# A linear-attention and gated-MLP block: the first two denominators on a bank pair of the queries, two gated rows in buffers of their own, one partial-product buffer for the late input pairs, and a new order table

## The chip, the cores and the metric

The kernel runs on one core of a Trainium2 chip. The engines named below are TensorE (PE, its weight loads PEld), VectorE (DVE), ScalarE (ACT), GpSimd (POOL) and SyncE (SP), which here issues nearly all transfers. The metric is the time of one execution in device microseconds; the lower, the better.

## The reference

The input x has 2048 rows of 512. Two residual blocks follow one another, the first a linear attention with 32 heads of 16, the second an MLP whose gate mixes the rows.

```python
phi = lambda t: where(t > 0, t + 1, exp(t)) + 1e-06
q, k, v = heads(layernorm(x) @ wqkv)
kv  = einsum('bhsd,bhse->bhde', phi(k), v);  z = einsum('bhsd->bhd', phi(k))
num = einsum('bhqd,bhde->bhqe', phi(q), kv); den = einsum('bhqd,bhd->bhq', phi(q), z)
h   = x + (num / den) @ wo
z   = gelu(layernorm(h) @ w_in);  z1 = z[..., :896];  z2 = layernorm(z[..., 896:])
g   = einsum('ts,bsf->btf', w_sp, z2) + b_sp
out = h + (z1 * g) @ w_out
```

The gelu is the tanh form; all inputs are bf16.

## The kernel before, in words

Rows come in 16 tiles of 128, or in 4 groups of 512 (GW). Everything between the loads and the last stores stays on the chip. The stages, with the times of the profile:

- 0 to 42: k units (two tiles each: norm, transposes, the product with wqkv, phi, then the outer product of pk and xn, L692) with the query units of the first two row groups between them. A query unit q_unit(tg, c) makes half of the queries of a row group, 2 × 128 columns, on two PSUM banks that next_pair() hands out by turns. It is named q12 and so on by tg and c. Its phi is an exponential on ACT (e), a clamp of e (L614) and a combination (L619) on DVE.
- 42 to 72: z_unit (L714) sums pk, DVE turns this into zc (zred, zT, zc, L718 to L721). The denominators: for each row group tg a product of zc and pqT (L824) on bank 6, its reciprocal on ACT by a logarithm (r) and an exponential (rcp), four SP transfers that spread rcp over the partitions (spread, L815), and two DVE multiplications of pqT (L840). Beside that: the four outer products are copied to ct by ACT, multiplied with the value columns of wqkv (L790), masked (kvm, L794) and multiplied with wo; the four results are copied to m by ACT and DVE (L801). Then, tile by tile, o_n: pqT times m, plus x by DVE (h, L852), row statistics by ACT (sh) and POOL, the norm by DVE (hn), and an SP transpose hnT.
- 72 to 140: the MLP's input products. Both w_in halves are multiplied by a scheme of two-by-two sums: hn_sums and w_sums build sums (hs, ws) on DVE; cell3 and cell2 run the products over a bank and its neighbour, ACT copies partial products into buffers p5z, and add_on (L882) adds them. cell2 makes z1 for two tiles at a time by z1_half: an ACT copy with gelu into z1t. The pairs of tiles 6, 7 and of 14, 15 (cell2_3 and cell2_7, the list ZLATE) come late, in the middle of the first mix block. Until then they alternated between p5z0 and p5z1.
- 105 to 212: the 2048 × 2048 mix in blocks mix(ia, ib, nest, early), the first of them early. The same two-by-two scheme is applied, partly twice (nested, with quarter sums nu of the weights, nv of z2 and adds at L1051). u_sums and comb (L755) build the weight sums in DVE, over the 16 transposed weight tiles wt. gate (L1019) and gate_p (L1030, L1031) add bias and the other partial result and multiply z1t in place; then an SP transpose makes zgT.
- 176 to 222: the output product with w_out, again by sums (us of zgT, vs of w_out by wout_sums), plus h, and stores.

The order of all operations on all engines is one table of numbers, ORDER, which schedule() decodes; waits follow from the data's hazards. So an engine runs its list in turn, and whatever waits holds up what is behind it. Many buffers share space: vs0 and vs1 lie where the upper parts of wt0 and wt1 were, and the nu buffers lie over wo and the space behind it.

Of the kernel before, what the change touches and what calls it, by code (L numbers as in the profile page):

```python
# [11 lines left out]
P = 128  # L12
GRAN = 16
EARLY = 0
SEM_NS = 45.0
# [1236 lines left out]
```

## Time and profile before

| | us |
|---|---|
| median of 3 runs (lowest, highest) | 224.12 (224.12, 224.31) |
| the profiled execution's own time | 224.06 |
| its span | 222.2 |
| busy PE, DVE, ACT, POOL | 215.1, 203.1, 142.7, 50.5 |
| granted TensorE clock | 1.00 |

The span runs from the first to the last instruction; the profiled run's own time has 1.9 us more around it. TensorE has 1334 matmul records of 1346, so a gap of about 0.2 us in a run of matmuls can be a record that is missing. In the rows of the timeline an engine's successive instructions overlap: of a DVE row of 0.62 us some 0.54 us pass until the next can start, of a TensorE group of 0.55 us some 0.39. In the chain of waits PE has 83% of the span, DVE 7%, ACT 3% and DMA 3%, of which 5.56 us are the first load of x.

### The profile page before, as it was taken

The numbers are of one execution on the slowest core, as the hardware profiler recorded it, in microseconds if no ns is written. First come the engines' busy times: TensorE is split into PE (matmuls) and PEld (weight loads), VectorE is DVE, ScalarE is ACT, GpSimd is POOL, SyncE is SP. The second block draws the span as 40 slices with busy tenths as digits, with TensorE's granted clock in tenths as the row PEclk, the third lists the DMA queues.
The fourth block names the chain that finished last, engine by engine and source line by source line (L and its number), as shares of the span: only waits on it lengthen the run. The fifth ranks groups of instructions, "written<-read, shape, count | busy, mean of one in ns | idle before, by whom it ended". The sixth has DMA issues, their size and how long they took to land.

```text
span 222.2 us, 3846 instructions
## 1 busy us (share of the span) xinstructions
PE 215.1 (97%) x1334; PEld 123.3 (56%) x1346; DVE 203.1 (91%) x472; ACT 142.7 (64%) x283; POOL 50.5 (23%) x133
## 2 busy tenths in 40 slices
PE   7999999999999999999999999999999999999995
PEld 6444444453334444444545555756766778767764
DVE  3899858969999999999999999997999998999895
ACT  5887654299789999999764646716385265533330
POOL 3444400000665655868700000000000000000000
PEclk9999999999999999999999999999999999999999
DMA  5758877928866553205994434986247024037274
GB/s 180 248 109 242 164 158 169 238 64 193 182 144 126 108 120 81 42 0 94 168 169 156 96 74 104 177 165 126 49 81 138 1 41 86 1 72 110 61 201 142
DMA packets 75026, 27.12 MB, mean 122 GB/s; under 512 B 64768, under 2 KB 75008, under 8 KB 75008
## 3 DMA queue, kind: packets, MB, share of 16 engines
q1 hardware_dynamic: 74304, 26.30, 55.7%
q10 hardware_dynamic: 704, 0.59, 0.8%
q8 instruction: 10, 0.16, 0.3%
q14 instruction: 8, 0.07, 0.1%
HBM read 6.95 MB, written 2.10 MB: 41 GB/s over the span
## 4 chain that ended last, share of the span: by engine, by line
PE 83%; DVE 7%; ACT 3%; DMA 3%; POOL 1%; issue 1%; SPq 1%
PE psum L434 77%; PE psum L692 5%; DMA x<-in_A_x_dram 3%; DVE st L543 2%; ACT e L453 1%; DVE h L852 1%; DVE h L1188 1%; DVE psum L882 1%; DVE pqT L619 1%; SPq L464 1%; DVE pqT L840 1%; DVE pk L619 1%; ACT z1t L453 0%; POOL st L569 0%; DVE e L614 0%
## 5 line engine op out<-in xcount | busy, mean ns | idle before, releaser
L453 ACT ACTIVATE psum<-psum 128x448 f32<-128x448 f32 (+2 forms) x76 | 31.1, 426 | 32.8 <-PE psum L434 21.8
L434 PE MATMUL psum<-z,wt 128*128 128x448 bf16 (+1 forms) x216 | 41.7, 335 | 0.1
L434 PEld LDWEIGHTS psum<-z,wt 128*128 128x128 bf16 x216 | 20.9, 98 | 15.4 <-DVE z L588 0.3
L434 PE MATMUL psum<-win,hnT 128*128 128x448 bf16 x112 | 26.4, 353 | 0.0
L453 ACT ACTIVATE z1t<-psum 128x448 bf16<-128x448 f32 (+1 forms) x24 | 16.4, 684 | 9.8 <-PE psum L434 7.6
L453 ACT ACTIVATE e<-psum 128x1024 bf16<-128x1024 f32 (+1 forms) x18 | 16.7, 929 | 9.2 <-PE psum L434 8.7
L434 PE MATMUL psum<-ws,hs 128*128 128x448 bf16 x72 | 18.9, 353 | 0.0
L434 PEld LDWEIGHTS psum<-win,hnT 128*128 128x128 bf16 x112 | 10.4, 98 | 11.0 <-ACT z L453 0.9
L434 PE MATMUL psum<-zt,sa 128*128 128x448 bf16 (+1 forms) x92 | 16.5, 316 | 0.0
L434 PE MATMUL psum<-m,pqT 128*128 128x512 bf16 x63 | 15.0, 380 | 1.0 <-DVE pqT L840 0.9
L882 DVE TENSOR_TENSOR psum<-psum,p5z 128x448 f32<-128x448 f32 x24 | 15.1, 628 | 0.6 <-ACT z1t L453 0.4
L453 ACT ACTIVATE z<-psum 128x896 bf16<-128x896 f32 x16 | 15.1, 979 | 0.7 <-PE psum L434 0.7
L692 PE MATMUL psum<-pk,xn 128*128 128x512 bf16 x63 | 15.2, 379 | 0.2 <-DVE pk L617 0.2
L434 PE MATMUL psum<-wqkv,xnT 128*128 128x512 bf16 x62 | 14.9, 379 | 0.4 <-DVE pqT L619 0.3
L434 PE MATMUL psum<-xnT,wqkv 128*128 128x512 bf16 x62 | 15.0, 379 | 0.2 <-issue 0.2
L453 ACT ACTIVATE p<-psum,b 128x448 f32<-128x448 f32 x22 | 13.2, 637 | 2.4 <-DVE u L1030 1.4
L1030 DVE TENSOR_TENSOR u<-psum,p 128x448 bf16<-128x448 f32 x22 | 13.6, 620 | 1.0 <-PE psum L434 0.6
L434 PE MATMUL psum<-nv,nu 128*128 128x224 bf16 x108 | 14.4, 259 | 0.1
L567 POOL TENSOR_SCALAR st<-st 128x1 f32<-128x1 f32 x10 | 4.8, 484 | 37.0 <-ACT sh L453 31.5
L543 DVE BATCH_NORM_STATS2 st<-x 128x6 f32<-128x512 bf16 x15 | 9.8, 678 | 3.7 <-DMA x<-in_A_x_dram 3.7
L434 PE MATMUL psum<-wout,zgT 128*128 128x256 bf16 (+1 forms) x71 | 12.8, 295 | 0.2
L614 DVE TENSOR_SCALAR e<-e 128x1024 bf16<-128x1024 bf16 (+1 forms) x18 | 6.9, 388 | 5.8 <-ACT e L453 5.8
(155 smaller groups left out, 459.7 us busy)
## 6 DMA issues: line engine op xcount, KB each, us to landing
r<-rcp SPq DMA_DIRECT2D x16, 128.0 KB, 2.8
out_dram<-h SPq DMA_DIRECT2D x15, 128.0 KB, 1.8
win<-in_B_w_in_dram SPq DMA_DIRECT2D x4, 448.0 KB, 3.8
x<-in_A_x_dram SPq DMA_DIRECT2D x6, 256.0 KB, 3.7
wqkv<-in_A_wqkv_dram SPq DMA_DIRECT2D x2, 512.0 KB, 4.9
wout<-in_B_w_out_dram SPq DMA_DIRECT2D x1, 896.0 KB, 5.0
wt<-in_B_w_sp_dram SPq DMA_TRANSPOSE x32, 4.0
wo<-in_A_wo_dram SPq DMA_DIRECT2D x1, 512.0 KB, 6.6
```

The lines of the kernel that those rows point to most:

```text
L434: inst = pe.matmul(out_ap, lhsT=a, rhs=b, start=start and i == 0, stop=stop and i == len(pairs) - 1, **kw)
L453: return g.add("ACT", lambda ac: ac.activation(out_ap, in_ap, func, **kw), [in_ap, *extra], [out_ap] + ([accum] if accum is not None else []),
L464: return g.add(eng, lambda q: q.dma_start(out_ap, in_ap), [in_ap], [out_ap], cost=issue, lat=lat, dma=name, **k)
L543: dve(lambda v: v.bn_stats(s[:, 0:6], src[:, n, :]), [src[:, n, :]], [s[:, 0:6]], D)
L567: pool(lambda p: p.tensor_scalar(s[:, 2:3], s[:, 0:1], s[:, 0:1], -1.0 / (n * n), op0=ALU.mult, op1=ALU.mult), [s[:, 0:1]], [s[:, 2:3]], 240)
L614: dve(lambda v: v.tensor_scalar(e, e, 1.0, EPS_PHI, op0=ALU.min, op1=ALU.add), [e], [e], w * GW, acc=4)
L619: dve(lambda v: v.scalar_tensor_tensor(dst, t, 1.0 + EPS_PHI, e, op0=ALU.add, op1=ALU.max), [t, e], [dst], w * GW, ps=True)
L692: inst = pe.matmul(bank(CB[c]), lhsT=xn[:, i, c * P:(c + 1) * P], rhs=pk[:, i, :], start=i == 0, stop=i == NT - 1)
L840: dve(lambda v, q=q, r=r: v.tensor_tensor(q, q, r, ALU.mult), [q, r], [q], 2 * GW, acc=2)
L852: dve(lambda v, n=n, b=b, s=s: v.scalar_tensor_tensor(h[:, n, :], bank(b), 1.0, x[:, n, :], op0=ALU.mult, op1=ALU.add, accum_out=s[:, 0:1] ...
L882: dve(lambda v: v.tensor_tensor(half(b), half(src), p, ALU.add), [half(src), p], [half(b)], HW, ps=True)
L1030: dve(lambda v: v.tensor_tensor(u, half(b), p, ALU.add), [half(b), p], [u], HW, ps=True)
```

## The change

Four edits, with no instruction more or less on any engine.

1. The denominator code becomes a function den(tg, db). Row groups 0 and 1 are now called ahead of the copies to ct, on the two banks that next_pair() gives; groups 2 and 3 follow the query units on bank 6, as before.
2. The gates of rows 8 and 9 in the early mix block write to buffers gt0 and gt1, and the transposes zgT8 and zgT9 read these. gt0 and gt1 lie where vs0 and vs1 are written later, so vs0 now follows the transpose of row 8, vs1 that of row 9. z1t8 and z1t9, whose space the copies z1t14 and z1t15 of the late pair take, are free earlier.
3. cell2_3 and cell2_7 both use p5z0; the nu1 buffers swap places by twos (k ^ 2).
4. A new ORDER table.

In the diff the code between the denominators and the query units (ct copies to m, L776 to L805) is left out where it only moves.

```diff
--- before.py
+++ after.py
@@ -13,7 +13,7 @@
 GRAN = 16
 EARLY = 0
 SEM_NS = 45.0
-ORDER = "c-jTQ0{|EY5Cp)zz5Up>8{4+i#<p#{v28WBZQHhO
+ORDER = "c-jrsg92EG76ibvyXVHXZQE&V+qP}nwr!hjY@2Ot
 
 
 class _Op:
@@ -350,6 +350,7 @@
     N4 = HT // 2 * (HW // 2) * 2
     o_up = [o_wsp + n * S * 2 + ZR for n in (0, 1, HT, HT + 1)]
     assert V3 + HF * P * 2 + ZR <= S * 2 and 2 * V3 + 8 * D + 4 * N4 + 2 * S // 2 <= NT * D * 2
+    gt = {HT + c: g.sbuf(f"gt{c}", o_up[c], [FH], BF16) for c in (0, 1)}
     vs = [g.sbuf(f"vs{k}", o_up[k], [HF, D // 2], BF16) for k in range(4)]
     us = [[g.sbuf(f"us{c}{k}", o, [HF, P], BF16) for k, o in enumerate(os)]
           for c, os in enumerate(([o + V3 for o in o_up], [o_pk + k * HF * P * 2 for k in range(4)]))]
@@ -357,7 +358,7 @@
     o_n = o_pk + 2 * V3 + 8 * D
     nv5 = [g.sbuf(f"nv5{k}", o_n + k * N4, [HT // 2, HW // 2], BF16) for k in range(4)]
     nv1 = [g.sbuf(f"nv1{k}", o_win + k * N4, [HT // 2, HW // 2], BF16) for k in range(4)]
-    nu1 = [g.sbuf(f"nu1{k}", o_wo + k * S // 2, [HT // 2, P], BF16) for k in range(4)]
+    nu1 = [g.sbuf(f"nu1{k}", o_wo + (k ^ 2) * S // 2, [HT // 2, P], BF16) for k in range(4)]
     np1 = g.sbuf("np1", o_ct + 3 * TB, [HW // 2], FP32)
     np5 = g.sbuf("np5", o_win + KD * FH * 2 + 3 * S, [HW // 2], FP32)
     assert o_ct + 3 * TB + HW * 2 <= cur[0] and 3 * S + HW * 2 <= KD * FH * 2 and S // 2 <= NT * 16 * 4
@@ -776,37 +777,7 @@
     u_sums(0, sae[:2])
     u_sums(1, sae[2:])
 
...
-    DB, MERGE, PM = 6, (), ()
+    MERGE, PM = (), ()
 
     def spread(tg, c, w):
         i = tg % 2
@@ -814,9 +785,8 @@
         src_ap = bass.AP(src.tensor, src.offset, [list(src.ap[0]), [0, 4], [1, w * GW]])
         g.add("SP", lambda q: q.dma_start(dst, src_ap), [rcp[:, i:i + w, :]], [dst], cost=700, lat=2200, dma=f"r{tg}{c // 2}")
 
-    for tg in range(NG):
+    def den(tg, db):
         tok = slice(tg * GW, (tg + 1) * GW)
-        db = DB
 
         def fn(pe, tok=tok, db=db):
             inst = None
@@ -838,6 +808,42 @@
                         pool(lambda v, q=q, r=r: v.tensor_tensor(q, q, r, ALU.mult), [q, r], [q], 1800)
                     else:
                         dve(lambda v, q=q, r=r: v.tensor_tensor(q, q, r, ALU.mult), [q, r], [q], 2 * GW, acc=2)
+
+
+    db = next_pair()
+    for tg in (0, 1):
+        den(tg, db + tg)
+
...
+    while qs:
+        q_unit(*qs.pop(0))
+    for tg in range(2, NG):
+        den(tg, 6)
 
 
     AB, HPAIR = [4, 5, 7], 2
@@ -1010,25 +1016,27 @@
     for q in ZPRE:
         cell2(q, win1, wq1[0], 6, 7, p5z[q % 2], z1_half)
 
-    def gate(n, c, b):
+    def gate(n, c, b, to=None):
         o = z1[n][:, c]
+        d = o if to is None else to[:, c]
         if GACT:
             u = u_t[cnt[0] % len(u_t)]
             cnt[0] += 1
             act(u, half(b), ACT.Identity, HW, bias=b32[:, n:n + 1], extra=[b32[:, n:n + 1]])
-            dve(lambda v: v.tensor_tensor(o, u, o, ALU.mult), [u, o], [o], HW, acc=2)
+            dve(lambda v: v.tensor_tensor(d, u, o, ALU.mult), [u, o], [d], HW, acc=2)
             return
-        dve(lambda v: v.scalar_tensor_tensor(o, half(b), b32[:, n:n + 1], o, op0=ALU.add, op1=ALU.mult),
-            [half(b), b32[:, n:n + 1], o], [o], HW, ps=True)
+        dve(lambda v: v.scalar_tensor_tensor(d, half(b), b32[:, n:n + 1], o, op0=ALU.add, op1=ALU.mult),
+            [half(b), b32[:, n:n + 1], o], [d], HW, ps=True)
 
     cnt = [0]
     GACT = True
 
-    def gate_p(n, c, b, p):
+    def gate_p(n, c, b, p, to=None):
         o, u = z1[n][:, c], u_t[cnt[0] % len(u_t)]
+        d = o if to is None else to[:, c]
         cnt[0] += 1
         dve(lambda v: v.tensor_tensor(u, half(b), p, ALU.add), [half(b), p], [u], HW, ps=True)
-        dve(lambda v: v.tensor_tensor(o, u, o, ALU.mult), [u, o], [o], HW, acc=2)
+        dve(lambda v: v.tensor_tensor(d, u, o, ALU.mult), [u, o], [d], HW, acc=2)
 
     HQ, H4 = HW // 2, HT // 2
 
@@ -1119,13 +1127,14 @@
             gate_p(tl, hi, E, pa)
             dma_t(zgT[tl], z1[tl], f"zg{tl}", issue=1300, lat=1750)
             matmuls(half(B), [(wt[th][:, s, :], z2[:, s, hi]) for s in ss], **onto)
-            gate_p(th, hi, B, pb)
+            to = gt[th] if early else None
+            gate_p(th, hi, B, pb, to)
             if nest & 16:
                 act(p2[c], half(B), ACT.Identity, HW, bias=b32[:, th:th + 1], extra=[b32[:, th:th + 1]])
                 continue
             matmuls(half(B), [(wt[th][:, HT + s, :], zt4[:, s, :]) for s in ss], **onto)
-            gate(th, lo, B)
-            dma_t(zgT[th], z1[th], f"zg{th}", issue=1300, lat=1750)
+            gate(th, lo, B, to)
+            dma_t(zgT[th], gt[th] if early else z1[th], f"zg{th}", issue=1300, lat=1750)
         if nest & 16:
             nested(SETS[0] + 2, SETS[1] + 2, wt[ia + HT][:, HT:NT, :], wt[ib + HT][:, HT:NT, :], zt4, nu2, nv4, np1)
             for i, c in sets:
@@ -1199,7 +1208,7 @@
         mix(MIX[k], MIX[k + 1], NEST[k // 2], k == 0)
         if k == 0:
             for q in ZLATE:
-                cell2(q, win1, wq1[0], 6, 7, p5z[q % 2], z1_half)
+                cell2(q, win1, wq1[0], 6, 7, p5z[0], z1_half)
             load_wout()
             for n in W4:
                 load_w(n)
```

What the new order does at three places. First ACT, from the query unit q12 on: ct are the copies of the outer products, e the exponentials of query units, r and rcp a denominator's two passes. Before:

```order
L453 ACTIVATE e_192<-psum 128x1024
L453 ACTIVATE ct<-psum 128x512 x4
L453 ACTIVATE e_192<-psum 128x1024
L453 ACTIVATE r<-psum,epst 128x512
L453 ACTIVATE rcp<-r 128x512
L453 ACTIVATE e_191<-psum 128x1024
L453 ACTIVATE r<-psum,epst 128x512
L453 ACTIVATE rcp<-r 128x512
```

Now:

```order
L454 ACTIVATE e_194<-psum 128x1024
L454 ACTIVATE r<-psum,epst 128x512
L454 ACTIVATE rcp<-r 128x512
L454 ACTIVATE r<-psum,epst 128x512
L454 ACTIVATE ct<-psum 128x512 x3
L454 ACTIVATE e_194<-psum 128x1024
L454 ACTIVATE ct<-psum 128x512
L454 ACTIVATE e_193<-psum 128x1024
L454 ACTIVATE rcp<-r 128x512
```

Both r and the first rcp moved ahead of the copies, and q22's exponential ahead of the fourth copy. On SP the spreads follow rcp. On DVE q12's phi moved ahead of zred, kvm behind q20's phi.

Second, DVE around the late pair of tiles 14 and 15; the two rows with p5z are its adds (cell2_7), gt0 the gate of row 8, nv are quarter sums. Before:

```order
L1019 TENSOR_TENSOR z1t8_69<-u0_134,z1t8_69 128x448
L755 TENSOR_TENSOR sa01_125<-sa00_124,wt2_82 128x1024
L1030 TENSOR_TENSOR u0_134<-psum,p511_131 128x448
L755 TENSOR_TENSOR nu52_172<-sa00_124,sa10_126 128x512
L755 TENSOR_TENSOR nv10_160<-z2_53 128x896
L755 TENSOR_TENSOR nv11_161<-z2_53,nv10_160 128x896
L755 TENSOR_TENSOR nv50_156<-zt0_77 128x896
L755 TENSOR_TENSOR nv51_157<-zt0_77,nv50_156 128x896
L1031 TENSOR_TENSOR z1t9_70<-u0_134,z1t9_70 128x448
L882 TENSOR_TENSOR psum<-psum,p5z1_133 128x448
L1019 TENSOR_TENSOR z1t9_70<-u1_135,z1t9_70 128x448
L755 TENSOR_TENSOR vs0_140<-wout_187 128x768
```

Now:

```order
L1026 TENSOR_TENSOR gt0_140<-u0_134,z1t8_69 128x448
L1038 TENSOR_TENSOR u0_134<-psum,p511_131 128x448
L1039 TENSOR_TENSOR gt1_141<-u0_134,z1t9_70 128x448
L756 TENSOR_TENSOR nu52_174<-sa00_124,sa10_126 128x512
L756 TENSOR_TENSOR nv10_162<-z2_53 128x896
L756 TENSOR_TENSOR nv50_158<-zt0_77 128x896
L756 TENSOR_TENSOR nv11_163<-z2_53,nv10_162 128x896
L756 TENSOR_TENSOR wt11_91<-wt3_83,wt11_91 128x1024
L756 TENSOR_TENSOR vs0_142<-wout_189 128x768
L888 TENSOR_TENSOR psum<-psum,p5z0_132 128x448
L756 TENSOR_TENSOR nv51_159<-zt0_77,nv50_158 128x896
L756 TENSOR_TENSOR nv12_164<-z2_53 128x896
```

The sum into wt11 and vs0 moved ahead of the pair's first add, nv51 and the last part of row 9's gate behind it; sa01 stands earlier, ahead of cell2_3's second add. On PE one short group of the mix (nu50) moved ahead of the group that waits for the first add, and one (nu11) ahead of the group that waits for the second. On SP the second part of wt7 now goes ahead of zgT8, and zgT9 behind four more weight loads.

Third, DVE in the second mix block (rows 7 and 4), around nu22, a quarter sum of wt7 and wt4; z1t10 is the gate of row 10. Before:

```order
L1019 TENSOR_TENSOR z1t10_71<-u2_136,z1t10_71 128x448
L755 TENSOR_TENSOR nv20_173<-z2_53 128x896
L755 TENSOR_TENSOR nu22_183<-wt7_87,wt4_84 128x512
L1030 TENSOR_TENSOR u1_135<-psum,p510_130 128x448
L755 TENSOR_TENSOR nu20_181<-wt4_84 128x512
```

Now:

```order
L1059 TENSOR_TENSOR psum<-psum,np5_171 128x224
L756 TENSOR_TENSOR sa10_126<-wt14_94 128x1024
L756 TENSOR_TENSOR nu12_168<-wt5_85,wt6_86 128x512
L756 TENSOR_TENSOR nu22_185<-wt7_87,wt4_84 128x512
L756 TENSOR_TENSOR nu52_174<-sa00_124,sa10_126 128x512
```

nu22 moved behind work of the third block (rows 5 and 6: wt5, wt6, wt14), while its product on PE moved ahead of the two long products of wt7 and wt15.

54 lines of the change are left out of this document (27 added, 27 removed).

## The prediction

> **What bounds the kernel now.** I read the totals first, then the chain of waits, then busy time by stage, then single stretches of the timeline.
>
> ```profile
> span 222.2 us, 3846 instructions
> PE 215.1 (97%) x1334; PEld 123.3 (56%) x1346; DVE 203.1 (91%) x472; ACT 142.7 (64%) x283; POOL 50.5 (23%) x133
> ```
>
> TensorE is busy in 97% of the span, VectorE in 91%. The change adds and removes no instruction on any engine, so all that it can win is time in which TensorE stands still, and all that it can lose is new standing still. Whether busy matmul time has slack of its own is read from one row:
>
> ```profile
> 132.68 1.68 PE L434 MATMUL psum<-zt,wt 128*128 128x448 bf16 x8
> 134.19 0.54 PE L434 MATMUL psum<-win,hnT 128*128 128x448 bf16 x2
> 134.94 0.55 PE L434 MATMUL psum<-zt,sa 128*128 128x224 bf16 x4
> 135.33 0.55 PE L434 MATMUL psum<-nv,nu 128*128 128x224 bf16 x4
> 136.03 0.55 PE L434 MATMUL psum<-win,hs 128*128 128x448 bf16 x2 [0.16 <-DVE psum L882]
> 137.18 0.55 PE L434 MATMUL psum<-z,wt 128*128 128x224 bf16 x4
> 137.89 0.55 PE L434 MATMUL psum<-ws,hnT 128*128 128x448 bf16 x2 [0.16 <-DVE psum L882]
> ```
>
> Eight matmuls of 448 columns take 134.19 − 132.68 = 1.51 us from start to start, 189 ns each: 2.4 columns per ns, hence no slack inside a group. A short group takes 0.39 (134.94 to 135.33). By that step the group at 136.03 could have started at 135.72 and the one at 137.89 at 137.57: two stalls of 0.32 each, both ended by the add of L882.
>
> The Trainium skill (Perfetto Trace Analysis, Identifying the Most-Contended Engine) warns that busy matmul time says little about the roofline and names the share of the weight loads instead. By that rule the 56% of PEld would leave room inside the 97%, and the sum would be free to fall by more than the stalls. The step of 189 ns speaks against it here.
>
> The chain shows where TensorE is not in front (start, us, what):
>
> ```profile
> 56.03 0.63 ACT sh L453 x2
> 57.10 1.05 POOL st L569
> 58.23 0.51 POOL st L570
> 58.82 0.59 POOL rs L583
> 59.84 1.83 DVE h L852 x6
> 62.93 71.81 PE psum L434 x372
> 134.77 0.55 ACT z1t L453
> 135.34 0.64 DVE psum L882
> ```
>
> Behind the head these are the two places: the denominators (51 to 63; the statistics of POOL, h and the scalings of L840 stand in front there) and the late input pair (134.8 to 137.9). By stage (PE, PEld, DVE, ACT, POOL busy, then clock, DMA share, GB/s):
>
> ```profile
> 41.00:63.00 22.00, 20.84 (x125) 8.46 (x126) 19.43 (x39) 17.73 (x32) 4.53 (x9) 1.00 0.73 155
> 125.00:140.00 15.00, 14.68 (x96) 8.71 (x94) 14.49 (x31) 8.58 (x19) 0.00 (x0) 1.00 0.54 107
> 140.00:160.00 20.00, 20.00 (x141) 13.33 (x139) 18.31 (x45) 8.70 (x20) 0.00 (x0) 1.00 0.68 128
> ```
>
> Here 22.00 − 20.84 = 1.16 us are lost on PE around the denominators and 0.32 in the late pair (the rows' ends are modelled, so the start-to-start sum, 0.64, is the better one). From 140 on PE loses nothing, and DVE has 1.69 us to spare.
>
> **Denominators.** Nothing new is computed; r, rcp and eight SP transfers move ahead of the ct copies.
>
> ```profile
> 17.00 1.90 PE L434 MATMUL psum<-wqkv,xnT 128*128 128x512 bf16 x7 [0.31 <-DVE pqT L619]
> 41.28 1.05 PE L714 MATMUL psum<-pk,ones 128*32 128x512 bf16 x16
> 42.53 0.68 DVE L718 TENSOR_REDUCE zred<-psum 128x128 f32<-128x512 f32 x1
> 43.59 0.29 DVE L721 TENSOR_TENSOR zc<-zT,selm 128x128 bf16<-128x128 f32 x1
> 44.20 2.07 ACT L453 ACTIVATE ct<-psum 128x512 bf16<-128x512 f32 x4 [2.65 <-PE psum L692]
> 46.12 1.05 ACT L453 ACTIVATE e<-psum 128x1024 bf16<-128x1024 f32 x1
> 47.03 0.72 ACT L453 ACTIVATE r<-psum,epst 128x512 f32<-128x512 f32 x1
> 47.78 0.63 ACT L453 ACTIVATE rcp<-r 128x512 bf16<-128x512 f32 x1
> 48.44 5.24 SPq L815 DMA_DIRECT2D r<-rcp  x8
> r<-rcp SPq DMA_DIRECT2D x16, 128.0 KB, 2.8
> 48.98 0.69 DVE L794 TENSOR_TENSOR kvm<-psum,bmask 128x512 bf16<-128x512 f32 x1
> 50.04 1.22 DVE L619 SCALAR_TENSOR_TENSOR pqT<-psum,e 128x1024 bf16<-128x1024 f32 x1
> 54.12 3.63 PE L434 MATMUL psum<-m,pqT 128*128 128x512 bf16 x16
> 58.10 1.04 PE L434 MATMUL psum<-m,pqT 128*128 128x512 bf16 x4 [0.36 <-DVE pqT L840]
> ```
>
> Before, eight issues take 5.24, so the fourth starts at 48.44 + 3 × 0.655 = 50.4 and lands some 2.8 later, at 53.2; the scaling of pqT after it lets o_0 start at 54.12. Now z_unit goes ahead of one product of k12 and starts near 40.2, with 0.2 won in the head (a product of 0.86 stands ahead of the group that waited for pqT at 17.00). DVE has q12's phi behind it by 41.7; zred to zc take 43.59 + 0.29 − 42.53 = 1.35, to 43.05; den_0 follows and r begins near 43.45, not 47.03. The transfers then land 3.6 earlier, by 49.7, and no longer bind. What binds instead: the copies start behind r, rcp and the second r, 0.72 + 0.63 + 0.72, the last of them from 44.7 on when den_1 is through, so the third ends near 46.9; q22's exponential (0.93 a step) is put ahead of the fourth, and the kv product starts near 48.4, against 48.2 for the same work before. On DVE kvm now stands behind q20's phi (1.22 and the short step on e ahead of it, 1.7 in all), and q22's phi is 0.5 late with its exponential: kvm starts near 51.1 and not at 48.98. Through wo's products and the m copies o_0 then starts near 54.55: 0.43 lost. Given back: the stall at 58.10 (DVE's scaling of the second quarter is done by then) and that before 62.93, 0.36 and 0.31 by the rows. But POOL's row statistics of o_0 begin behind an ACT pass that is now preceded by q32's second pass and q30's exponential (the 0.63 of sh ends near 57.4 and not at 56.6), and 1.05 + 0.51 + 0.59 and gaps bring the norm to 60.1, where DVE holds it ahead of o_2's h and the next scalings. So o_8 and o_9 together end near 64.6, against 64.67: −0.05, the 0.2 of the head included. Bounds: −0.55 if the norm doesn't hold DVE up, +0.4 if only o_0's lag counts. I take −0.05, since both queues are followed there row by row.
>
> The Trainium skill (PSUM — Partial Sum Buffer, PSUM bank collisions raise a hardware error) asks that two engines never meet on a bank. By that rule the borrowed query pair has a price: q22's matmuls must wait until ACT has read both denominators. By the rows r of the second ends at 45.4, as q22's second half comes up; the rule's wait is then nil, and 0.7, one r, if PE comes that much sooner.
>
> **Gate buffers, one partial buffer, nu swap.** Copies into z1t14 and z1t15 no longer wait for transposes:
>
> ```profile
> ACT z1t L453 <- DMA zgT<-z1t: 0.4, 1, 0.4
> zgT<-z1t SPq DMA_TRANSPOSE x16, 2.9
> 129.59 1.68 PE L434 MATMUL psum<-z,wt 128*128 128x448 bf16 x8
> ```
>
> That one wait of 0.4 had idle ACT time around it: 0. In exchange vs0 on DVE waits for the transpose of row 8 out of gt0, with the late pair's adds behind it. gate 8 ends near 131.0, the transfer behind one weight load on SP lands 2.9 later, near 134; vs0 comes up near 134.8: also 0, but 1.0 if the landing is as late as 135.8. The late pair's first add: from the end of wt9's product (129.59 + 1.68 = 131.3) DVE has to do four steps of 0.54 (one add, three nv), 0.32, 0.33, 0.60 (the wt11 sum) and 0.47 (vs0), 3.88 in all, to 135.2; the copy by ACT ends at 134.77 + 0.55 = 135.3, so the add still starts at 135.34. On PE one short group more stands ahead of each of the two waiting groups, 0.39 each, more than each stall of 0.32. Value: −0.64; bounds −0.64 and +0.2 (the add 0.87 later, as its place among DVE's rows alone would have it, less the 0.64).
>
> **The rest of the order.** Small swaps in 64 to 125 and 140 to 222 move producers by up to 1 us against consumers that had 0.05 to 0.5 of slack. DVE's gap below covers those after 155; for those before I put +0.1, bounds 0 and +0.6.
>
> **Sum.** The profiled run took 224.06 (span 222.2, so 1.9 around it): −0.05 − 0.64 + 0.1 = −0.59, 223.47; the median of 224.12 is 0.06 above that run, so 223.5.
>
> **Rivals.**
>
> ```profile
> 155.80 0.39 DVE L1019 TENSOR_TENSOR z1t<-u,z1t 128x448 bf16<-128x448 bf16 x1 [1.58 <-ACT u L453]
> 156.64 0.42 DVE L755 TENSOR_TENSOR nu<-wt,wt 128x512 bf16<-128x512 bf16 x1
> 170.68 0.55 PE L434 MATMUL psum<-nv,nu 128*128 128x224 bf16 x4
> ```
>
> *DVE late in the second mix block (slower).* nu22 of that block moves 10.8 us of DVE work down, its product on PE 3.0 us up. If DVE keeps its idle 1.58 at the row-10 gate, nu22 ends at 156.64 + 0.42 + 10.8 = 167.9, while PE comes for it at 167.65 less the 0.7 won: 0.9 late; the gate of row 4, moved 2.1 down and its consumer 0.4 down, then brings it to 1.5. Net +0.8: 224.9. For: DVE is 91% busy and everything there is just in time. Against: 2.9 us more of DVE work stand ahead of that gate now, which should fill the 1.58. It decides once more than 0.65 of it stays idle.
>
> *The late pair keeps its stalls (no change).* If the transpose of row 8 or the 3.88 us of DVE work run 0.3 late, PE stalls as before: −0.05 + 0.1, 224.2. For: 14.49 of 15 us busy on DVE; against: the sum above.
>
> *The norm doesn't bind (faster still).* Then −0.55 in place of −0.05: 223.0.
>
> **Chances.** Forecast 0.47, DVE late 0.30, stalls kept 0.14, norm free 0.09. About 0.2% (0.45 us) is what a measurement can tell from none, so faster begins under 223.67: 0.41 of the forecast and 0.09 make 0.50; 0.06 and 0.08 are the same; 0.30 and 0.06 slower. The range, 222.8 to 225.1, holds all but the ends of the outer cases; the forecast's own is 223.1 to 224.1.
>
> **What would show it.** Right: r ahead of ct on ACT near 43.4, o_0 near 54.5, no stall at 58.1, the two gaps at L882 gone, no idle 1.58 on DVE, PE at 20.0 of 20 after 140. Wrong: DVE waiting for zgT8 at vs0, PE waiting for nu22 near 168, or any new gap over 0.5 between 64 and 125.

## The result, and the profile after

The changed kernel took 223.26 us (223.06 to 223.64), the kernel before 224.22 beside it: ratio 0.9957, 95% interval 0.9944 to 0.9969. The forecast was 223.5. A second measurement with other runs (after_rep below) gave 223.44, ratio 0.9960, interval 0.9945 to 0.9975.

The totals of the profile after, then busy time by stage (us, then PE, PEld, DVE, ACT, POOL busy, clock, DMA share, GB/s):

```profile
span 221.6 us, 3862 instructions
PE 216.4 (98%) x1346; PEld 123.1 (56%) x1346; DVE 202.6 (91%) x472; ACT 142.6 (64%) x283; POOL 51.1 (23%) x133
```

```profile
41.00:63.00 22.00, 21.56 (x128) 8.41 (x120) 19.42 (x39) 16.84 (x29) 4.31 (x9) 1.00 0.68 147
125.00:140.00 15.00, 15.00 (x102) 9.35 (x100) 14.38 (x32) 8.46 (x19) 0.00 (x0) 1.00 0.53 99
140.00:160.00 20.00, 20.00 (x136) 13.01 (x135) 19.47 (x48) 8.90 (x20) 0.00 (x0) 1.00 0.87 153
```

PE's busy time around the denominators rose from 20.84 to 21.56, in the late pair from 14.68 to 15.00. The first rise, 0.72, is more than was won there: 12 matmul records are missing from the profile before and none from this one, and the table below gives 0.16. The late pair on PE (start, us, group):

```profile
135.17 0.55 PE L435 MATMUL psum<-zt,sa 128*128 128x224 bf16 x4
135.55 0.55 PE L435 MATMUL psum<-nv,nu 128*128 128x224 bf16 x4
135.93 0.54 PE L435 MATMUL psum<-win,hs 128*128 128x448 bf16 x2
136.31 0.54 PE L435 MATMUL psum<-ws,hs 128*128 128x448 bf16 x2
136.69 0.55 PE L435 MATMUL psum<-z,wt 128*128 128x224 bf16 x4
137.07 0.55 PE L435 MATMUL psum<-nv,nu 128*128 128x224 bf16 x4
137.46 0.55 PE L435 MATMUL psum<-zt,sa 128*128 128x224 bf16 x4
137.84 0.54 PE L435 MATMUL psum<-ws,hnT 128*128 128x448 bf16 x2
```

Every step is 0.38 or 0.39: the two gaps ended by the add are gone. The group of nu50 stands ahead of the first waiting group now (135.55), those of nu11 and of the second sa00,zt0 ahead of the second (137.07 and 137.46).

Spans alone don't show where time was won, since the first loads land differently from execution to execution. So the rows of each trace were matched with those of the profile before, group by group, and at places behind which both orders have done the same TensorE work, the ends of that work were compared. The table gives by how much TensorE is later (+) or earlier (−) than in the profile before, in us, at nine such places (times of the profile before):

| profile | 40 | 65 | 93 | 101 | 134 | 145 | 185 | 195 | 218 |
|---|---|---|---|---|---|---|---|---|---|
| changed kernel | 0.33 | 0.17 | 0.20 | −0.16 | −0.16 | −0.82 | −0.85 | −0.57 | −0.53 |
| changed kernel again (after_rep) | −0.05 | −0.21 | 0.23 | −0.14 | −0.13 | −0.79 | −0.82 | −0.51 | −0.48 |
| den_old | 0.07 | 0.07 | 0.11 | −0.24 | −0.24 | −0.89 | −0.92 | −0.62 | −0.57 |
| late_old | −0.08 | −0.23 | −0.19 | −0.55 | −0.54 | 0.21 | 0.19 | 0.47 | 0.51 |
| mid_old | 0.07 | −0.09 | 0.04 | | 0.04 | −0.61 | −0.64 | −0.61 | −0.59 |
| tail_fix | −0.41 | −0.56 | −0.50 | −0.86 | −0.85 | −1.51 | −1.53 | −1.45 | −1.40 |
| ct_dve | 0.47 | 0.23 | 0.67 | 0.31 | 0.33 | −0.33 | −0.35 | −0.33 | −0.30 |
| best | −0.12 | −0.36 | −0.24 | −0.60 | −0.51 | −1.16 | −1.19 | −1.14 | −1.11 |

A row is read by its differences. The changed kernel wins 0.16 between 40 and 65 (denominators), 0.36 between 93 and 101, 0.66 in the late pair, and gives back 0.28 between 185 and 195; with the small steps between, 0.86 from 40 to 218. Its first profile stood 0.33 late already at 40, its second waited 0.39 once at 68, without which it wins 0.82. Neither occurs in both profiles, though the program is the same; the last section comes back to the wait at 68.

### The profile page after: what moved, and what is told of

The parts are those of the page before. It is cut to its first block, busy times and chain, and to the rows that moved or that the text cites. A ratio compares the mean times of both kernels' runs of the same rounds, so it can differ in the third digit from the quotient of the medians.

```text
span 221.6 us, 3862 instructions
## 1 busy us (share of the span) xinstructions
PE 216.4 (98%) x1346; PEld 123.1 (56%) x1346; DVE 202.6 (91%) x472; ACT 142.6 (64%) x283; POOL 51.1 (23%) x133
## 4 chain that ended last, share of the span: by engine, by line
PE 81%; DVE 12%; DMA 3%; ACT 2%; SPq 1%; issue 0%
PE psum L435 76%; PE psum L693 4%; DMA x<-in_A_x_dram 3%; DVE st L544 2%; DVE pqT L620 2%; DVE e L615 1%; DVE pk L620 1%; DVE pqT L810 1%; ACT ct L454 1%; ACT r L454 1%; DVE h L858 1%; SPq L465 1%; DVE m L839 1%; PE psum L715 0%; ACT e L454 0%
## 5 line engine op out<-in xcount | busy, mean ns | idle before, releaser
L435 PE MATMUL psum<-win,hnT 128*128 128x448 bf16 x112 | 25.8, 352 | 0.0
L435 PE MATMUL psum<-wout,zgT 128*128 128x256 bf16 (+1 forms) x77 | 15.0, 302 | 0.0
L888 DVE TENSOR_TENSOR psum<-psum,p5z 128x448 f32<-128x448 f32 x24 | 14.6, 620 | 0.4 <-ACT z1t L454 0.3
L568 POOL TENSOR_SCALAR st<-st 128x1 f32<-128x1 f32 x10 | 3.6, 362 | 36.5 <-ACT sh L454 31.4
L435 PEld LDWEIGHTS psum<-zt,sa 128*128 128x128 bf16 x92 | 8.9, 98 | 4.4 <-ACT psum L454 0.2
```

Source lines behind the costliest of these rows:

```text
L435: inst = pe.matmul(out_ap, lhsT=a, rhs=b, start=start and i == 0, stop=stop and i == len(pairs) - 1, **kw)
L568: pool(lambda p: p.tensor_scalar(s[:, 2:3], s[:, 0:1], s[:, 0:1], -1.0 / (n * n), op0=ALU.mult, op1=ALU.mult), [s[:, 0:1]], [s[:, 2:3]], 240)
L888: dve(lambda v: v.tensor_tensor(half(b), half(src), p, ALU.add), [half(src), p], [half(b)], HW, ps=True)
```

## The experiments

| kernel | median, us (range) | ratio to before, 95% |
|---|---|---|
| changed kernel, first measurement | 223.26 (223.06 to 223.64) | 0.9957, 0.9944 to 0.9969 |
| den_old | 223.19 (222.91 to 223.33) | 0.9953, 0.9941 to 0.9965 |
| den_only | 225.54 (224.82 to 225.74) | 1.0057, 1.0044 to 1.0069 |
| head_old | 223.56 (223.04 to 223.98) | 0.9973, 0.9964 to 0.9981 |
| late_old | 224.79 (224.66 to 225.09) | 1.0030, 1.0019 to 1.0040 |
| late_only | 224.07 (223.72 to 224.69) | 0.9994, 0.9978 to 1.0010 |
| late_nogt | 224.76 (224.03 to 225.13) | 1.0021, 1.0006 to 1.0037 |
| late_gt | 229.36 (227.16 to 230.89) | 1.0206, 1.0168 to 1.0245 |
| mid_old | 223.51 (223.30 to 224.37) | 0.9969, 0.9952 to 0.9985 |
| ct_dve | 222.93 (222.70 to 224.12) | 0.9941, 0.9925 to 0.9958 |
| tail_fix | 223.00 (222.71 to 223.49) | 0.9946, 0.9930 to 0.9962 |
| after_rep | 223.44 (223.16 to 223.56) | 0.9960, 0.9945 to 0.9975 |
| best | 222.92 (222.67 to 223.59) | 0.9942, 0.9921 to 0.9963 |

The kernel before took 224.20, 224.27 and 224.24 in the three groups of runs.

### Denominators: den_old and den_only

den_old, in the changed kernel:

```diff
-    db = next_pair()
-    for tg in (0, 1):
-        den(tg, db + tg)
...
-    for tg in range(2, NG):
-        den(tg, 6)
+    for tg in range(NG):
+        den(tg, 6)
```

with the order of before from 43 to 67 us. den_only is the reverse: the kernel before with this code and this stretch of the changed order.

> The changed kernel with all four denominators back behind the query units on bank 6, as before, and with the order of before between 43 and 67 us on all engines; the head, the buffers and everything from 67 us on as changed. Theory (the early denominators give back ahead of o_0 what they win behind it): o_0 starts near 54.1 again, the idle stretches at 58 and 63 come back, o_8 and o_9 end within 0.2 of the changed kernel's at 64, and the time is 223.3 to 223.5. Rival (the early denominators are worth their 0.55): 223.8.

> The kernel before with the early denominators alone: their code, and the order of the changed kernel between 43 and 67 us on all engines; head, buffers, late pair and everything behind as before. Theory (early denominators about nil, late pair all): 224.0 to 224.3, within 0.2 of before's 224.22, with the two gaps of the late pair at 136 and 138 as before. Rival (early denominators worth 0.5): 223.7. The head's order is that of before, so the third input transfer of the issue queue shows whether its later landing in the changed kernel (8.44 against 7.74) belongs to the order.

den_old keeps 0.07 from 40 to 65: TensorE runs through the stage as before, with the waits at 58 and 63. The changed kernel wins 0.16 there, and 223.19 against 223.26 and 223.44 says that this can't be seen in the time. The theory stands in its rows (its time, 223.3 to 223.5, was 0.1 too high), and the rival's 223.8 does not. den_only missed on both sides: it is 1.3 slower than the kernel before. Its PE and DVE rows:

```profile
44.25 0.40 PE L793 MATMUL psum<-pqT,zc 128*32 128x512 bf16 x4 [1.29 <-DVE zc L721]
```

```profile
41.70 1.23 DVE L619 SCALAR_TENSOR_TENSOR pqT<-psum,e 128x1024 bf16<-128x1024 f32 x1
42.84 0.68 DVE L718 TENSOR_REDUCE zred<-psum 128x128 f32<-128x512 f32 x1
43.91 0.29 DVE L721 TENSOR_TENSOR zc<-zT,selm 128x128 bf16<-128x128 f32 x1
```

With the old head, q12's phi ends at 42.93 on DVE, zc follows at 44.20, and the denominator, now the next thing on TensorE, stands for 1.29 us. TensorE goes from 0.34 ahead of the profile before at 40 to 0.86 behind it at 93. So the early denominators alone lose, and with the head's moves (z_unit and q12 sooner) they come out about even.

### The head: head_old and after_rep

head_old takes from the changed kernel the order of its first 19 us and puts the old one there (k_unit_0's e and pk, the order of POOL's constants, and so on); after_rep changes nothing.

> The changed kernel with the order of before in the first part of the program (the first 19 TensorE, 19 VectorE, 13 ACT and 28 POOL instructions, up to about 19 us), everything else as changed. TensorE stood 0.69 us behind the kernel before at 8 us in the changed kernel's profile and 0.3 behind from 22 to 42. Theory (that lag is the input transfers' landing in that one execution, not the order): the time stays at 223.26 within 0.2, and the landing varies from profile to profile of the same order. Rival (the new order in the head costs what the profile shows): 0.3 faster, 222.95.

> The changed kernel itself, for a second profile and beside the others of this call. Theory (the 0.69 that its first profile shows at 8 us and the 0.33 from 22 to 42 are the landing of the input transfers in that one execution): this profile stands elsewhere at 22 us, anywhere from 0.5 ahead of to 0.4 behind the kernel before, and is the same from there on; the median is 223.1 to 223.4. Rival (they belong to its order): 0.3 behind again.

Three transfers of x issued by SP in the first profile of the changed kernel, then in its second:

```profile
2.17 6.07 SPq L465 DMA_DIRECT2D x<-in_A_x_dram  x3
```

```profile
2.18 5.39 SPq L465 DMA_DIRECT2D x<-in_A_x_dram  x3
```

The same issues in the same order ended 0.67 apart. At 40 us the eight profiles with the new head stand between 0.41 ahead of and 0.46 behind the profile before, the five others with the old one between 0.34 ahead and 0.61 behind. So the lag of the first profile is that execution's. head_old isn't faster: 223.56 lies 0.30 above the changed kernel's 223.26, outside the 0.2 of the theory, and 0.12 above its 223.44. The rival, 0.3 faster, falls; whether the new head is worth anything, these runs can't tell.

### The late pair: late_old, late_only, late_nogt, late_gt

late_old, on PE of the changed kernel (hs3 and ws03 are the groups that wait for the adds):

```diff
 mix_2 psum<-sa00,zt0
-mix_2 psum<-nu50,nv50
 cell2_7 psum<-hs3,win1
 cell2_7 psum<-hs2,ws02
+mix_2 psum<-nu50,nv50
 mix_2 psum<-wt2,z2
-mix_2 psum<-nu11,nv11
 mix_2 psum<-sa00,zt0
 cell2_7 psum<-hnT,ws03
+mix_2 psum<-nu11,nv11
```

> The changed kernel with the two short TensorE groups that it moved up in the late input pair put back behind the two groups that add the partial buffer (nu50 behind hs2, nu11 behind ws03, and the one ACT copy that goes with it); buffers and everything else as changed. Theory (the late pair's fillers carry the win): both stalls of 0.32 us ended by the add of the partial buffer come back at 136 and 138, TensorE at about 14.7 of 15 us busy between 125 and 140, and the time is 223.9, 0.6 above the changed kernel's 223.26. Rival (slack behind absorbs it, or the win came from elsewhere): the stalls come back in the rows but the time stays within 0.2 of 223.26.

It lost more than the theory said, 1.35 to 1.53 against the changed kernel, and only one of the two old stalls came back. Its PE rows with gaps:

```profile
135.50 0.55 PE L435 MATMUL psum<-win,hs 128*128 128x448 bf16 x2 [0.17 <-DVE psum L888]
...
137.51 0.56 PE L435 MATMUL psum<-zt,sa 128*128 128x224 bf16 x4 [0.31 <-ACT np L454]
...
139.27 0.56 PE L435 MATMUL psum<-z,nu 128*128 128x224 bf16 x4 [0.43 <-ACT psum L454]
```

The first gap (0.33 from start to start beyond the step) is the old one. The other two (0.48 and 0.60) are new: the nested groups are copied by ACT behind them, and moved down they bring the copies, and the next groups that need these, down with them. Together 1.41. So late_old shows that the fillers' places matter, but it does not measure what they are worth alone.

late_only tries the reverse on the kernel before: one partial buffer, the nu swap, nu10 and nu11 early on DVE, nu50 and nu11 moved up on PE.

> The kernel before with the late pair alone: one partial-product buffer, the nu buffers swapped, nu10 and nu11 made on VectorE at about 122 and 125 us (as in the changed kernel), and the groups nu50 and nu11 moved up on TensorE ahead of the two groups that wait for the adds, with nu50's ACT copy; no gate buffers, all else as before. Theory (the late pair alone carries 0.64 to 0.66): both gaps at 136 and 138 are gone and the time is 223.55, 0.65 under before's 224.2. Rival (it needs the rest of the changed order, the gate buffers above all): one gap stays or turns up within 3 us behind it, and the time is 224.0 to 224.2.

The rival's time and its remaining gap came true, though not for the reason it put first, the gate buffers. The first gap goes, the second stays:

```profile
138.01 0.55 PE L434 MATMUL psum<-ws,hnT 128*128 128x448 bf16 x2 [0.17 <-DVE psum L882]
```

In taking nu50 from between the two waiting groups and putting nu11 there, the edit left the second gap one group short: the changed order also has the second sa00,zt0 ahead of ws03. 0.30 more is lost at 139.08, where nu51 on DVE comes only behind ws03.

late_nogt therefore takes all 13 groups of PE's new order from nu10 to nu51, with nu13 early on DVE; late_gt adds the gate buffers, moves the second gate of row 9 behind nv52 on DVE, and SP's transpose of row 9 to its new place.

> The kernel before with the whole TensorE order of the late pair (its 13 groups from nu10 to nu51 as in the changed kernel), one partial-product buffer, the nu buffers swapped, nu10, nu11 and nu13 early on VectorE; no gate buffers. Theory (the gate buffers carry part of the win, which the prediction put at nothing): the two gaps before hs3 and ws03 go, but the group wt7,z2 now comes up at 139.2 and waits for the copy into z1t15, which waits for the transpose of row 9 out of z1t9, landing at 139.2 and copied by 139.9: a new gap of 0.6 there, and the time is 224.1 to 224.2, as before. Rival (gate buffers worth nothing): no gap there, 223.6.

> The same as late_nogt, and with it the gate buffers, the second gate of row 9 moved down on VectorE from ahead of the second late add to behind the window sum nv52, and row 9's transposes at the changed kernel's place on the issue queue. Theory: the copy into z1t15 no longer waits, no gap over 0.2 from 135 to 141, and the time is 223.6, 0.6 under before's 224.2. Rival (it needs the rest of the changed order around it on VectorE): a gap of 0.3 or more stays, 223.9 or more.

late_nogt shows the gap that the theory named. PE, then ACT:

```profile
139.90 0.56 PE L434 MATMUL psum<-z,wt 128*128 128x224 bf16 x4 [0.53 <-ACT z1t L453]
...
141.27 0.56 PE L434 MATMUL psum<-nv,nu 128*128 128x224 bf16 x4 [0.43 <-ACT psum L453]
```

```profile
139.30 0.54 ACT L453 ACTIVATE z1t<-psum 128x448 bf16<-128x448 f32 x1 [1.10 <-DMA zgT<-z1t]
```

ACT stands for 1.10 until row 9's transpose has landed out of z1t9, and 0.69 of it reaches PE. The time, 224.76, is even above the expected 224.2: a second gap of 0.60 comes at 141.27, where nu52 follows nu51 at once, without the long product that the changed kernel has between them.

late_gt has no gap at that product. Up to 141 it goes from 0.59 behind the profile before to 0.13 ahead, 0.72 won; then comes the gap at nu52, and a long one that neither theory expected. DVE, PE, then busy time by window:

```profile
146.87 0.56 DVE L756 TENSOR_TENSOR vs<-wout,vs 128x768 bf16<-128x768 bf16 x1 [3.13 <-DMA zgT<-gt]
```

```profile
148.39 0.93 PE L435 MATMUL psum<-nv,wt 128*128 128x224 bf16 x4 [3.30 <-DVE psum L1054]
```

```profile
145.00:147.00 2.00, 0.10 (x1) 0.00 (x0) 0.14 (x1) 0.63 (x1) 0.00 (x0) 1.00 1.04 175
147.00:148.00 1.00, 0.00 (x0) 0.00 (x0) 1.00 (x3) 0.00 (x0) 0.00 (x0) 0.70 0.89 202
148.00:154.00 6.00, 5.61 (x18) 2.58 (x19) 4.66 (x13) 0.53 (x1) 0.00 (x0) 0.50 0.37 61
154.00:160.00 6.00, 6.00 (x37) 3.46 (x36) 4.72 (x12) 1.68 (x3) 0.00 (x0) 0.98 0.62 128
```

vs1 lies where gt1 lies, and the experiment left vs1 at its old place on DVE (142.9 in the profile before): it waited 3.13 for the transpose of row 9 out of gt1, with everything behind it. The changed order has vs1 at 173.5. So the gate buffers have a price, which the order pays by moving vs1 behind the transposes. No run adds the whole of the late pair to the kernel before without a stall of its own; that it is worth 0.66 rests on the rows of the changed kernel.

### 93 to 101 us: mid_old

The order of before between 77 and 109 us on PE, DVE, ACT and POOL, the rest as changed.

> The changed kernel with the order of before between about 77 and 109 us on all engines (92 to 156 on TensorE, 119 to 203 on VectorE, 85 to 115 on ACT, 59 to 120 on POOL); all else as changed. Theory (this stretch, where both profiles count TensorE as 100% busy, holds small waits of 0.04 to 0.10 in the order of before that add up to the 0.33 us by which the changed kernel pulls ahead between 93 and 101): 223.6, 0.33 slower than the changed kernel. Rival (the busy sum is right and nothing is lost there): 223.26.

PE before (first four rows), and after:

```profile
96.61 0.54 PE L434 MATMUL psum<-ws,hs 128*128 128x448 bf16 x2
97.06 0.55 PE L434 MATMUL psum<-win,hnT 128*128 128x448 bf16 x2
97.44 0.54 PE L434 MATMUL psum<-ws,hs 128*128 128x448 bf16 x2
97.86 0.99 PE L434 MATMUL psum<-win,hnT 128*128 128x448 bf16 x4
```

```profile
96.33 0.54 PE L435 MATMUL psum<-ws,hnT 128*128 128x448 bf16 x2
96.71 0.54 PE L435 MATMUL psum<-ws,hs 128*128 128x448 bf16 x2
97.09 0.54 PE L435 MATMUL psum<-ws,hnT 128*128 128x448 bf16 x2
```

No row has an idle time, and the busy sum of this stretch is full in both. But groups of two take 0.45, 0.38, 0.42 from start to start in the one, 0.38 each in the other: a row's modelled end reaches 0.16 past the point where the next group can start, and waits below that vanish in it. Five such waits of 0.04 to 0.10, at 95.09, 97.06, 97.86, 98.30 and 99.13, make 0.33 of the 0.36. (The changed order has one of its own just behind the table's place, 0.13 at 100.62, and wins that back in small steps by 134.) mid_old has them again (it stays at 0.04 from 93 to 134, where the changed kernel goes from 0.20 to −0.16), but in its one profile the loss between 185 and 195 is 0.03 and not 0.28 (the next part comes back to this), so that the net is small; 223.51 lies 0.07 to 0.25 above the changed kernel, between the theory and the rival. Shown is the place, not its worth in the time.

### Beyond the change: ct_dve, tail_fix, best

ct_dve, in the changed kernel, with the two copies ahead of ws02 on DVE:

```diff
-    QSPLIT, KSPLIT, CACT = (6, 7), (0, 2), 2
+    QSPLIT, KSPLIT, CACT = (6, 7), (0, 2), 1
```

tail_fix, on DVE:

```diff
 mo_pair_1 h<-psum,tmp10
-nv41<-zt2,nv40
 mo_pair_1 h<-psum,h
 mo_pair_1 h<-psum,tmp11
-nv43<-zt2,nv41
+nv41<-zt2,nv40
 mix_5 psum<-psum,np1
 mo_pair_2 tmp00<-psum,h
 mo_pair_2 tmp01<-psum,h
+nv43<-zt2,nv41
```

best has both edits.

> The changed kernel with two of the four ct copies (the second and fourth column block) moved from ACT to VectorE, ahead of the last window sum, in VectorE's idle 2.41 us before q22's exponential; all else as changed. Theory (ACT's row r, rcp, r, three ct copies is what TensorE and VectorE wait for between 45 and 58): q22's exponential starts near 47.05 and not 47.41, the kv product at 48.7 and not 49.00, o_0 0.4 earlier, and the time is 222.85, 0.4 under the changed kernel's 223.26. Rival (VectorE's row from 48.5 to 64 is full whatever its start, and POOL's statistics and the norm hold it): o_0 earlier, but the end of o_8 and o_9 and the time as in the changed kernel, 223.1 to 223.3.

> The changed kernel with two quarter sums on VectorE moved down: nv41 from between the two h adds of the second output pair to behind them, nv43 from ahead to behind the two tmp steps of the third; all else as changed. Theory (those two rows of 0.53 us hold up the h add, the ACT copy behind it and the tmp step for which TensorE waits 0.19 at 192.2 and 0.08 at 189.5): both gaps go and the time is 223.0, 0.27 under the changed kernel's. Rival (the tail waits for the transposes of the last gated rows, landing at 210.9): the gaps go, the wait at 211.35 grows by as much, and the time stays at 223.26.

> The changed kernel with both edits: two ct copies on VectorE and the two quarter sums of the tail moved down. Theory by the rows of the single edits (0.2 of the tail's 0.27 was won; the copies win 0.07 at the end of the o tiles): 223.0, 0.27 under the changed kernel in this call. Rival by the medians of the single edits (0.33 and 0.26): 222.7.

ct_dve's DVE and PE rows:

```profile
48.40 0.43 DVE L615 TENSOR_SCALAR e<-e 128x1024 bf16<-128x1024 bf16 x1 [0.99 <-ACT e L454]
```

```profile
50.14 1.90 PE L435 MATMUL psum<-xnT,wqkv 128*128 128x512 bf16 x8 [0.22 <-DVE pqT L620]
```

That profile stood 0.13 later at 40, so q22's exponential on ACT came 0.20 sooner and not 0.36: ACT now waits for q22's second product, which itself waits for the second denominator's r on its bank. At 65 us 0.08 is left of it. In the rows of this stage that is the rival, yet the median is 0.3 to 0.5 under the changed kernel's, below the rival's 223.1. (The profiled execution, 224.12, is the slowest of the twelve: it stood 0.47 late at 40 and waited 0.38 at 68.)

The table shows the rest. ct_dve loses only 0.02 between 185 and 195, where the changed kernel loses 0.28. One DVE instruction makes the difference, nu21, a quarter sum. In the changed kernel, then in mid_old and in ct_dve:

```profile
187.52 0.42 DVE L756 TENSOR_TENSOR nu<-nu,wt 128x512 bf16<-128x512 bf16 x1 [0.28 <-PE psum L435]
```

```profile
187.38 0.43 DVE L756 TENSOR_TENSOR nu<-nu,wt 128x512 bf16<-128x512 bf16 x1
```

```profile
187.66 0.42 DVE L756 TENSOR_TENSOR nu<-nu,wt 128x512 bf16<-128x512 bf16 x1
```

DVE stands for 0.28 to 0.30 before it in six profiles (the changed kernel's two, den_old, head_old, late_old, tail_fix) and not at all in three (mid_old, ct_dve, best), though the order around it is the same. The profile puts the wait down to TensorE, whose short group from 186.90 to 187.45 ends just before; but in mid_old the same group ends at 187.66, behind the start of nu21, so nu21 doesn't need it. In the three the edits further up changed the number of instructions ahead of it in DVE's list, waits counted: it stands one place earlier in mid_old and two later in ct_dve and best. Whether the place is the cause is not shown. But 0.08 and 0.26 make 0.34, the lower end of what the medians say.

tail_fix: PE after, then with the fix:

```profile
191.71 0.49 PE L435 MATMUL psum<-vs,us 128*128 128x256 bf16 x3
192.23 0.50 PE L435 MATMUL psum<-wout,zgT 128*128 128x256 bf16 x3
```

```profile
191.03 0.49 PE L435 MATMUL psum<-vs,us 128*128 128x256 bf16 x3
191.36 0.49 PE L435 MATMUL psum<-wout,zgT 128*128 128x256 bf16 x3
```

The step goes from 0.52 to 0.33, 0.19 won, although DVE's wait before nu21 is there in this profile too, and it lasts to the end (−1.53 at 185, −1.40 at 218, where the changed kernel loses 0.32): the wait at 211 didn't grow. The 0.08 at 189 stays; that step waits for the h add ahead of nv41. But the step is 0.34 in mid_old and ct_dve without the fix, so the fix removes what the wait before nu21 costs there, and where that wait is absent it has nothing left to win. best fits this: it loses 0.05 between 185 and 195, and its 222.92 is no better than ct_dve's 222.93. It beats the kernel before (0.9921 to 0.9963); against the changed kernel, 223.44 in the same group of runs, its interval overlaps, and by the rows it wins 0.99 from 40 to 218 where the changed kernel wins 0.82 to 0.86.

## Why the prediction was right, point by point

**The sum.** 0.59 was forecast; 0.96 and 0.80 were measured, 0.86 and 0.82 by the rows. The mechanism was right in its largest term, the late pair. The first term came near by two errors that offset, and the last one is a win and a loss that the prediction did not name and that nearly cancel.

**Denominators (−0.05).** Near in total, and partly by luck. The −0.05 holds 0.2 won in the head, and so 0.15 lost behind it. No win in the head can be told, and behind it 0.16 was won between 40 and 65, none of it visible in the time. The steps, in the first profile (which stood 0.33 late there): ACT, then PE.

```profile
44.01 0.69 ACT L454 ACTIVATE r<-psum,epst 128x512 f32<-128x512 f32 x1 [3.86 <-PE psum L794]
...
45.39 0.69 ACT L454 ACTIVATE r<-psum,epst 128x512 f32<-128x512 f32 x1
45.98 1.56 ACT L454 ACTIVATE ct<-psum 128x512 bf16<-128x512 f32 x3
47.41 1.05 ACT L454 ACTIVATE e<-psum 128x1024 bf16<-128x1024 f32 x1
48.31 0.63 ACT L454 ACTIVATE ct<-psum 128x512 bf16<-128x512 f32 x1
```

```profile
50.23 1.90 PE L435 MATMUL psum<-xnT,wqkv 128*128 128x512 bf16 x8 [0.17 <-DVE pqT L620]
...
55.15 2.87 PE L435 MATMUL psum<-m,pqT 128*128 128x512 bf16 x12
58.20 1.90 PE L435 MATMUL psum<-m,pqT 128*128 128x512 bf16 x8 [0.17 <-DVE h L858]
```

r came at 44.01 (forecast 43.45 plus the 0.33: 0.2 late), o_0 at 55.15 (54.55 plus 0.33: 0.3 late), and the stall at 58 halved where it should have gone. Both misses have one source: DVE is full from 48.49 on, and everything in it follows q22's exponential, which stands behind r, rcp, r and three copies on ACT. The bank rule that was weighed there (the Trainium skill, PSUM — Partial Sum Buffer, PSUM bank collisions raise a hardware error) costs what the rows gave it, nearly nothing: q22's second product started at 46.13, behind the end of the second r at 46.08, and 0.08 after the 46.05 that its first half's step gives. The give-back behind o_0 came, less what stayed of that stall. In the head the gap at 17.00 went, and 0.42 turned up at 22.5, where k4's outer product waits for pk.

**Late pair (−0.64).** Measured −0.66, in both profiles. But "gate buffers: 0" was wrong as a reason. The prediction looked for waits that the old addresses caused in the old order and found one, hidden. late_nogt shows that in the new order the same wait costs 0.69: the buffers win nothing and are what lets the fillers stand there. The one partial buffer belongs here too: it frees the space under nu10 and nu11, so that nu11 is made at 125 and not at 137.9, after the add for which PE waited.

**The rest of the order (+0.1).** Wrong in its parts: −0.36 between 93 and 101, +0.28 to +0.31 between 185 and 195. The first was read as nothing to win because the stage's busy time was full. The second is DVE's wait of 0.28 before nu21 with the quarter sums behind it, which no row of the profile before gives away; with other instruction counts ahead of it (mid_old, ct_dve) it is 0.02 to 0.03, so that the term as a whole came near the forecast is chance.

**Rivals.** The late pair kept no stall. The norm was ready at 60.11, as forecast, but DVE's full row came to it only at 60.22: it didn't bind, and the 0.55 of that rival didn't follow either, since DVE was full ahead of it too. DVE late in the second mix block did not come true: of the idle 1.58, 0.28 was left, and PE was 20.00 of 20 busy; nu22 ended at 166.57, 0.28 before PE took it, so that rival was near. The 0.28 after 185 is also a loss by DVE, but not one of this kind: it comes and goes with the wait before nu21, while up to that wait TensorE and DVE stand equally far apart (both 0.21 later in mid_old).

**The rule of the Trainium skill** (Perfetto Trace Analysis, Identifying the Most-Contended Engine) that weight loads, beside the share of peak matmul work, tell the headroom better than matmul busy time was weighed against the 189 ns step. The trace bears out the step: the time fell by waits between groups, no group's step became shorter (448 columns still take 1.51 us for eight), and PEld stands at 56% before and after. The rule's warning about matmul busy time holds in another sense: rows look longer than their step, and hid 0.36 us.

## What to carry to other kernels

When the busy share of a pipelined engine is full, compare starts with starts, group by group, before calling a stretch free of waits. A buffer that removes no wait in the old order can be what the new order stands on, so price it in the new one, and look for whoever is written to its space next. And when one part of a hand-set order is undone or taken over, take its whole chain (fillers, the copies behind them, the groups that need the copies), or the experiment measures a stall of its own making. Before a fix is credited with a gap that it closes, look whether kernels without the fix have that gap at all.

## What the runs showed of the hardware that was not expected

In late_gt PE stood still for 3.30 us, from 145.1 to 148.4, and the granted clock was 0.70 in the slice from 147 to 148, 0.50 from 148 to 154 and 0.98 from 154 to 160 (rows above). Eight matmuls of 448 columns take 1.51 us from start to start elsewhere; here two such products and a short group ran from 148.39 to 154.66. At half the rate for some 6 us that costs about 3 us more than the stall itself. One of its runs kept a mean clock of 1.000 and took 227.16, 2.9 above the kernel before; the others had 0.985 to 0.993 and took 229.1 to 230.9. The Trainium skill (TensorE: Matmul & The Clock Gate, Part 1: The HAM clock gate) describes this: half rate after an idle window of about 3.4 us, full rate after a busy one. The trace agrees in the halving and differs in the lengths: the drop came about 2.3 us into a pause that was 3.3 us long in all, and the return only after 5.8 us of work.

The transfers of the first input rows end up to 0.7 us apart from one execution to the next, with the same program; two profiles of single executions can't be compared in the head more closely than that. The four issues of the last spread vary as well: they took 2.64 and 3.57 us in the two profiles of the changed kernel, and 2.64 to 3.57 over all that have its order. In the two profiles with the early denominators where they took 3.54 and 3.57 (ct_dve and after_rep), TensorE waited 0.38 and 0.39 at 68 us. In den_old, with the old order in this stage, they took 3.54 too and TensorE did not wait. So the early denominators seem to leave less slack there, which may be why their 0.16 is not seen in the time; that, and what makes the transfers longer, is open.
